# Chunked attention followed by a snake MLP on one core: another order of the words of the four MLP passes

## The chip, the cores and the metric

The kernel runs on one core of one Trainium2 chip. The metric is the device time of one execution in microseconds (us); lower is better. A profile is a separate execution, recorded by the hardware profiler; its span is the time from the first to the last recorded instruction, and the execution's own time is a little longer.

## The reference

Attention over four batches, eight heads, 768 positions of 64 values. Each chunk of 32 queries sees 8 memory rows, 16 positions to its left, itself and 8 to its right. The result, 3072 tokens of 512 values, goes through an MLP with a periodic activation.

```python
# attention, for each chunk c of 32 queries
k_full = np.concatenate([mem_k, k_ctx], axis=2)
v_full = np.concatenate([mem_v, v_ctx], axis=2)
scores = (1.0 / np.sqrt(64)) * np.matmul(q_c, k_full.transpose(0, 1, 3, 2))
a = np.exp(scores - scores.max(-1, keepdims=True))
out[:, :, c_start:c_end] = np.matmul(a / (a.sum(-1, keepdims=True) + 1e-09), v_full)
# MLP: x (3072, 512), w_in (512, 2048), w_out (2048, 512)
h = x @ w_in
s = np.sin(alpha * h)
g = h + s * s / (alpha + 1e-09)
return g @ w_out
```

## The kernel before

**Stages.** The program is a front and four passes. The front does the attention of batch 0. Pass i (0 to 3) does the MLP of batch i, and within it the attention of batch i+1 (pass 3 has none). The order of everything is written out by hand as five strings of words, `WORDS` (L21): the first is the front, the other four are the passes. `Stage.run` (L558) takes the words of a string one after the other and calls `do_` plus the first letter; the rest of the word is its argument. Each word emits instructions at the end of the queues of the engines that it uses. Every engine runs its own queue in order; between engines there are only the waits that the data ask for. So a word's place in the string sets its place in each queue.

**The MLP's first half.** The 2048 hidden values are 16 tiles of 128. For a tile n, `b` takes a pair of PSUM banks and does the matmuls of the first 384 columns, 4 of 384 columns each (L457), `h` the other 384 and then the sine on ScalarE (L472), `q` the square with the engine as its last letter (A is ScalarE at L477; V VectorE and P GpSimd, both at L480), and `g` the combination with the matmul result on VectorE (L484), which writes a slice of `gT` and gives the pair of banks back. There are four pairs. Tile buffers `u` and `s` are four deep as well.

**The second half.** `o` opens a feed of 96 matmuls of 512 columns (L495) for six blocks of 128 tokens, and `f` with a number takes so many from the feed. Whatever a pass leaves is taken at the end. After the 16 matmuls of a block, a copy out of PSUM (L502) on the engine that `e` names in turn, and an output transfer on SyncE's queue.

**The attention of the next batch.** `l` and `k` turn a quarter of q and k on TensorE (L312), `L` and `K` copy the results (L332, L323); these are for batch 1. Batches 2 and 3 have their k and q rows loaded by GpSimd's queue (`R`, with a count: L268 and L274 for k, L281 for q, 16 and 6 issues for a batch) into `kst` and `q_bf`, and crossed over by SyncE's queue (`X`, with a count: L296 to kT, L299 to qT, 8 and 6 for a batch). `V` loads a range of heads of v (batch, first head, last head); `m` and `H` put the memory rows of v into place (`H` by eight copies on GpSimd, L231), `Z` those of k. `s` with one to three digits does the scores of those blocks of 96 queries (L418) and the exponentials (three on ScalarE for a block, L432), `v` the values of one block (L447) and their normalisation on VectorE (L386, L387). The block is then transposed into `xT`, the input of the next pass, either by TensorE and a copy (`t` on VectorE, `T` on ScalarE, L399 and L402) or by a transfer on SyncE's queue (`c`, L666). The first column half of a tile needs blocks 0 to 3, the second blocks 4 to 7.

**The others.** `I` and `U` load pieces of w_in and w_out on GpSimd's queue. `W` (L738) is a one-element sine or exponential on ScalarE, which makes the engine load the table of that function there (ACT_TABLE_LOAD); without it, the table is loaded ahead of the first real sine or exponential. `d` loads rows for later batches.

**Slots.** PSUM banks, pairs and the six `x_blk` buffers are given out by the order in which they were returned (`Banks`, L95, and `Slots`, L81), so another order of words gives other banks too. Each of the two kinds of transfer queue has eight completion semaphores in rotation: an issue waits until the transfer eight issues earlier on it has landed.

Of the kernel before, what the change touches and what calls it, by code (L numbers as in the profile page):

```python
# [26 lines left out]
    ),  # L27
    (
# [5 lines left out]
    ),  # L34
    (
# [5 lines left out]
    ),  # L41
    (
# [5 lines left out]
    ),  # L48
    (
# [3 lines left out]
    ),  # L53
)

# [833 lines left out]
```

## Time and profile before

| what | us |
|---|---|
| median of 3 runs (lowest, highest) | 215.34 (215.27, 215.65) |
| the profiled execution's own time | 214.68 |
| its span | 212.8 |
| TensorE matmul busy (1772 instructions) | 204.9 |
| VectorE busy (210) | 139.9 |
| ScalarE busy (229) | 143.7 |
| GpSimd busy (142) | 100.9 |

The granted TensorE clock is 1.00 throughout. A matmul's record covers its whole way through the array, and matmuls overlap each other, so a busy TensorE does not show by itself that no time is lost. What tells is the time between the first matmuls of two stretches against the number of matmuls between them. The pieces of the chain of waits ("the chain that ended last") give such starts with counts. The front is before about 25 us; pass 0 begins at 24.8 us, pass 1 at 74.9, pass 2 at 121.5 and pass 3 at 167.6. The last 112 matmuls of the second half run from 188.8 us.

### The profile page before, as it was taken

To read this page: it belongs to the slowest core of one execution; us is meant where nothing else is said; L and a number is where in the kernel's file an instruction comes from. 1 tells how busy PE (TensorE), PEld (TensorE's weight loads), DVE (VectorE), ACT (ScalarE), POOL (GpSimd) and SP (SyncE) were. 2 spreads that over 40 slices of the span, in tenths; PEclk is the share of its full clock that TensorE was granted. 3 is DMA by queue.
4 is the path that set the end of the run, shared out by engine and by line. 5 is a ranking of instruction groups with operands and counts; after the bars stand their busy time and mean duration, and the time that the engine had idled before them with its cause. 6 is when DMAs were issued, how large, how long until landed. Compare 5 with 4: busy or idle time off the path is not lost.

```text
span 212.8 us, 4568 instructions
## 1 busy us (share of the span) xinstructions
PE 204.9 (96%) x1772; PEld 118.1 (55%) x1772; DVE 139.9 (66%) x210; ACT 143.7 (68%) x229; POOL 100.9 (47%) x142
## 2 busy tenths in 40 slices
PE   7879999999999999999999999999999999999994
PEld 7456665565455556555455555554555555554453
DVE  4788788999452749976766649897247187865010
ACT  2579898978848469968837199887856189891110
POOL 8998605589697297109795048664000022200000
PEclk9999999999999999999999999999999999999999
DMA  5999999999999999999999259999944400000312
GB/s 156 332 158 139 212 207 204 205 139 183 131 160 155 176 114 129 121 144 146 146 152 183 74 125 125 137 157 133 134 104 107 137 0 0 3 2 0 148 52 99
DMA packets 95853, 27.82 MB, mean 131 GB/s; under 512 B 84808, under 2 KB 92376, under 8 KB 95832
## 3 DMA queue, kind: packets, MB, share of 16 engines
q0 software_dynamic: 69152, 13.64, 89.3%
q1 hardware_dynamic: 25720, 12.68, 29.6%
q10 hardware_dynamic: 960, 1.21, 1.7%
q8 instruction: 14, 0.23, 0.6%
q14 instruction: 7, 0.06, 0.1%
HBM read 29.66 MB, written 6.29 MB: 169 GB/s over the span
## 4 chain that ended last, share of the span: by engine, by line
PE 78%; DVE 8%; ACT 5%; DMA 4%; issue 3%; SPq 1%; DVEq 0%; ACTq 0%
PE ps L495 39%; PE ps L457 30%; DMA kq_f<-in_k_dram 4%; PE ps L447 3%; DVE gT L484 2%; PE ps L418 2%; DVE x_blk L387 2%; DVE s L480 2%; ACT s L477 2%; PE ps L399 1%; ACT pt L365 1%; PE ps L312 1%; ACT u L472 1%; DVE q_bf L686 1%; DVE rinv L386 0%
## 5 line engine op out<-in xcount | busy, mean ns | idle before, releaser
L495 PE MATMUL ps<-w_out_sb,gT 128*128 128x512 bf16 (+1 forms) x400 | 89.1, 371 | 0.0
L457 PE MATMUL ps<-xT,w_in_sb 128*128 128x384 bf16 x512 | 85.9, 326 | 0.6 <-DVE gT L484 0.4
L484 DVE SCALAR_TENSOR_TENSOR gT<-s,inv_alpha,ps 128x768 bf16<-128x768 f32 x64 | 63.1, 1012 | 12.3 <-ACT s L477 5.2
L457 PEld LDWEIGHTS <-w_in_sb 128*128 128x128 bf16 x512 | 49.7, 98 | 35.2 <-issue 2.0
L472 ACT ACTIVATE u<-ps,alpha_sb 128x768 f32<-128x768 f32 x64 | 56.6, 894 | 16.9 <-PE ps L457 14.4
L495 PEld LDWEIGHTS <-gT 128*128 128x128 bf16 x400 | 37.1, 98 | 37.1 <-DVE gT L484 0.2
L480 POOL TENSOR_TENSOR s<-u 128x768 f32<-128x768 f32 x11 | 17.2, 1568 | 67.2 <-ACT u L472 56.4
L432 ACT ACTIVATE pt<-ps,biasm 128x256 bf16<-128x256 f32 x72 | 27.1, 488 | 10.5 <-PE ps L418 10.5
L502 DVE COPY o_sb<-ps 128x512 f32<-128x512 f32 (+1 forms) x15 | 10.0, 669 | 27.6 <-PE ps L495 25.7
L480 DVE TENSOR_TENSOR s<-u 128x768 f32<-128x768 f32 x23 | 21.9, 953 | 7.6 <-ACT u L472 7.5
L477 ACT ACTIVATE s<-u 128x768 f32<-128x768 f32 x30 | 25.0, 841 | 0.5
L387 DVE TENSOR_TENSOR x_blk<-ps,rinv 96x512 bf16<-96x512 f32 x32 | 22.0, 687 | 1.1
L502 ACT COPY o_sb<-ps 128x512 f32<-128x512 f32 (+1 forms) x10 | 5.7, 572 | 22.0 <-PE ps L495 22.0
L208 POOL DMA_DIRECT2D vw<-in_v_dram x13 | 12.0, 926 | 6.3 <-PE ps L399 5.4
L386 DVE RECIPROCAL rinv<-ps 96x8 f32<-96x8 f32 x32 | 6.4, 199 | 13.1 <-PE ps L447 12.7
L215 POOL DMA_DIRECT2D vw<-in_v_dram x13 | 13.3, 1024 | 1.6 <-DMA vw<-in_v_dram 1.6
L274 POOL DMA_DIRECT2D kst<-in_k_dram x16 | 13.0, 815 | 1.8 <-DMA vw<-in_v_dram 1.2
L268 POOL DMA_DIRECT2D kst<-in_k_dram x16 | 11.1, 691 | 2.1 <-DMA kst<-in_k_dram 1.0
L281 POOL DMA_DIRECT2D q_bf<-in_q_dram x12 | 10.7, 911 | 0.0
L402 ACT COPY xT<-ps 128x384 bf16<-128x384 bf16 x10 | 5.0, 496 | 8.2 <-PE ps L399 8.2
L447 PEld LDWEIGHTS <-pt 128*128 128x128 bf16 x192 | 8.2, 97 | 4.2 <-ACT pt L432 0.3
L447 PE MATMUL ps<-vw,pt 128*128 128x65 bf16 x192 | 8.9, 193 | 0.0
(83 smaller groups left out, 140.7 us busy)
## 6 DMA issues: line engine op xcount, KB each, us to landing
out_dram<-o_sb SPq DMA_DIRECT2D x23, 256.0 KB, 2.2
q_bf<-in_q_dram POOLq DMA_DIRECT2D x12, 128.0 KB, 7.7
kq_f<-in_k_dram SPq DMA_DIRECT2D x3, 384.0 KB, 6.2
kq_f<-in_q_dram ACTq DMA_DIRECT2D x3, 384.0 KB, 7.9
w_in_sb<-in_moe_w_in_dram POOLq DMA_DIRECT2D x1, 1152.0 KB, 12.9
vw<-in_v_dram POOLq DMA_DIRECT2D x7, 128.0 KB, 7.7
vw<-in_v_dram POOLq DMA_DIRECT2D x8, 112.0 KB, 8.1
kst<-in_k_dram POOLq DMA_DIRECT2D x14, 64.0 KB, 5.5
```

Source lines behind the costliest of these rows:

```text
L215: nc.gpsimd.dma_start(vw[72:128, c0:hi, 0:D], win(vflat, base + QW * c0 + 48, hi - c0, 56))
L274: nc.gpsimd.dma_start(kst[72:72 + n, j, :].rearrange("p (h d) -> p h d", d=D), k[b, :, QW * j + 48:QW * j + 48 + n, :].rearrange("h p d -> ...
L387: nc.vector.tensor_tensor(out=x_blk[:].rearrange("p g e d -> p e g d"), in0=otv[0:QW, :, :, 0:D], in1=rinv[:].unsqueeze(3).to_broadcast([Q ...
L432: nc.scalar.activation(pt[:, 0:H * QW].rearrange("p (g e c) -> p g e c", g=2, e=4)[:, :, :, 32 * m:32 * m + 32], sc[:, :, 0:4 * QW].rearra ...
L447: nc.tensor.matmul(otv[:, e, hp, :], pt[:, QW * i:QW * i + P], vws[b % 2][:, 2 * hp + e, j, 0:D + 1],)
L457: nc.tensor.matmul(t["hT"][:, hf, 0:HALF], w_in_sb[:, kt, P * t["ft"]:P * t["ft"] + P], t["xT"][:, kt, HALF * hf:HALF * hf + HALF], start= ...
L472: nc.scalar.activation(t["u"][:], t["hT"][:, :, 0:HALF], ACTF.Sin, scale=alpha_sb[:, ft:ft + 1])
L477: nc.scalar.activation(s2[:], u[:], ACTF.Square)
L480: e.tensor_tensor(out=s2[:], in0=u[:], in1=u[:], op=ALU.mult)
L484: nc.vector.scalar_tensor_tensor(out=gT[:, ft, :].rearrange("p (e c) -> p e c", e=2), in0=t["s2"][:], scalar=inv_alpha[:, ft:ft + 1], in1= ...
L495: nc.tensor.matmul(o[:, c0:c1], gT[:, ft, P * s:P * s + P], w_out_sb[:, ft, c0:c1], start=(ft == 0), stop=(ft == FT - 1),)
L502: copier(state["engines"][state["o"] % len(state["engines"])])(o_sb[:, c0:c1], o[:, c0:c1])
```

## The change

The four strings of the passes are replaced. The front's string and all functions are the same. TensorE does the same 1772 matmuls and the same number of every form. Counted over the program, ScalarE has 31 squares where it had 30, VectorE 20 where it had 23, and GpSimd 13 where it had 11; one of the K copies goes from VectorE to ScalarE and one copy of a transposed block from ScalarE to VectorE; 13 one-element activations become 8; the table is loaded 8 times in both. The tiles are opened (`b`) in the same order as before in all four passes; the second half of a tile (`h`) changes places with the next tile's `b` at a few (tiles 4 and 3 in pass 0, 7 and 11 in pass 1, 6 and 7, and 13 and 14 in pass 2). In pass 0 the squares stay with their engines, and `s70` goes ahead of `s61`. In pass 1, `R4` goes ahead of `V226`, the squares of tiles 11 and 13 go from ScalarE to GpSimd and that of 12 from GpSimd to ScalarE, and blocks 0, 5 and 1 are scored together. In pass 2, `H3` goes ahead of `R16`, `V305` goes ahead of `V357` and ahead of the square of tile 14; the squares of tiles 6, 9, 3 and 14 are GpSimd's and only those of 0, 2 and 12 VectorE's. In pass 3 the square of tile 6 goes from ScalarE to VectorE, that of 13 from VectorE to ScalarE and that of 15 from ScalarE to GpSimd.

```diff
--- before.py
+++ after.py
@@ -26,30 +26,28 @@
         'I02 Cs T00 v21 t10 T20 t31 z1 t11 I27 t21 Ws '
     ),
     (
-        'o8 b0 h0 I7g q0V U69 U12 b1 h1 dq108 q1A b4 h4 b3 g0 h3 b6 g1 dk108 q4V g4 q3A b2 h2 h6 b5 h5 Ufg g3 '
-        'b7 q2V U01 U56 q6P h7 g2 q5A b10 U24 q7P g6 h10 b9 q10A g5 h9 U45 b8 h8 g7 g10 q8A q9V V158 b11 h11 '
-        'g9 b13 g8 h13 l0 l2 l3 L0A L2A q13P k2 q11V Ube b15 U9b g11 Uef g13 K2V h15 b12 q15V h12 q12A b14 '
-        'g15 f7 h14 V125 k1 k0 g12 l1 K1V k3 L1V L3A q14V K3A K0A V102 dy f9 g14 s61 f16 m1 s70 s3 f13 v0 f3 '
-        'v6 Z2 c6 f6 v3 f5 s542 T3 f10 T0 v4 f6 v2 f2 v1 c4 c2 f7 v7 f1 T1 f3 v5 Ws T7 f8 t5 '
+        'I7g b0 U69 Ws h0 q0V dq108 b1 h1 o8 b4 b3 q1A h4 g0 g1 h3 q4V b6 dk108 q3A g4 U24 U12 b2 h2 h6 b5 g3 '
+        'h5 q2V b7 U01 q5A g2 U56 q6P h7 U45 b10 g6 h10 b9 g5 q7P q10A g7 h9 b8 h8 b11 g10 V158 q9V U9b q8A '
+        'h11 b13 g9 h13 l0 l2 g8 q13P Ube l3 Ufg L0A L2A q11V g11 g13 k2 b15 h15 b12 K2A q15V g15 h12 b14 '
+        'q12A Uef V125 h14 f7 l1 k1 g12 k0 K0A k3 K3A L3V L1A V102 q14V f9 K1V s70 g14 m1 f16 s61 s3 f11 v0 '
+        'dy v6 f8 c6 f1 v3 T0 f3 s542 T3 Z2 f11 v4 f9 c4 v2 v7 v1 f3 c2 f12 T1 v5 f6 t5 t7 '
     ),
     (
-        'b0 o1 h0 b3 R2 q0V h3 b1 Ws q3A g0 g3 h1 q1V b2 R4 h2 q2A b5 h5 b4 h4 Ws g1 g2 q5V g5 b6 q4A h6 R8 '
-        'Ws g4 b8 q6A g6 h8 R1 b9 q8V h9 b7 q9A g8 h7 R3 V378 b11 h11 V226 b10 g9 R4 h10 V202 V268 q7V Ws '
-        'q10A f2 X8 q11A g7 f8 b12 h12 g10 g11 b14 h14 q12P g12 b13 h13 q13A g13 q14A f7 X6 Z3 b15 g14 h15 f7 '
-        'eV We s24 q15V f6 g15 f7 s05 s1 f1 m2 f14 v4 v1 f6 v0 f1 v2 f2 c4 f6 s63 s7 t1 f4 c2 v6 T0 f4 v3 f4 '
-        'v7 c7 v5 t3 f17 t5 T6 '
+        'R4 b0 h0 o1 q0V b3 h3 q3A b1 h1 b2 h2 g0 g3 b5 q2A q1V R2 R1 h5 b4 g1 h4 g2 q5V b6 g5 q4A h6 b8 g4 '
+        'q6A h8 b9 g6 h9 q8V b7 R8 g8 q9A R3 b11 h7 V378 R4 h11 b10 g9 h10 f8 V268 q7V V226 V202 X8 q11P g7 '
+        'b12 q10A h12 g10 g11 b14 q12A h14 g12 b13 h13 f9 q14A q13P eV X6 g13 b15 h15 g14 q15V g15 f6 s24 f2 '
+        'Z3 f12 s051 m2 f10 v4 f7 v1 c4 f4 v0 s63 We T1 f6 v2 f4 s7 t0 v5 f8 v3 c2 f4 v6 v7 c7 t3 f16 t5 T6 '
     ),
     (
-        'b3 R16 H3 Ws b0 h0 h3 b5 h5 Ws b1 q5A q0V g0 q3P R6 g3 X4 h1 Ws q1A b2 h2 X4 g5 g1 b4 h4 b6 q4A q2V '
-        'h6 X2 g2 b7 h7 b9 h9 X1 g4 X1 q6V b8 g6 X2 eV o1 h8 q7P g7 q8A b11 h11 q11A q9P b10 g9 g8 h10 b13 '
-        'g11 h13 q10V g10 b14 h14 b12 q13P V357 V305 h12 g13 q12V q14A f8 eAV b15 g12 h15 f6 g14 q15V s24 f16 '
-        'g15 f2 s103 f9 v4 v0 f3 f2 c4 v3 f2 c3 v2 f1 c2 f6 c0 s675 f10 v1 f4 c1 Ws f1 v7 v5 c7 v6 f2 c6 c5 '
-        'f24 '
+        'H3 b3 b0 h0 h3 b5 h5 R16 q0V g0 b1 q3P o1 X4 q5A h1 b2 R6 q1A h2 g3 b4 g5 h4 g1 b6 q2V g2 q4A b7 g4 '
+        'h6 h7 X4 q6P b9 h9 b8 g6 q7A h8 g7 X1 b11 q8A q9P h11 eV X2 g9 q11A b10 g8 h10 q10A X1 b13 g11 b14 '
+        'h13 q13A b12 V305 g10 g13 h12 h14 q12V g12 f6 q14P V357 b15 h15 X2 q15A eAV f4 g14 We f4 s24 g15 f18 '
+        's103 f9 We v4 c4 f2 v0 c0 f3 v2 f4 We v3 f4 c3 c2 s675 f10 v1 f5 c1 v7 c7 v6 v5 c6 c5 f27 '
     ),
     (
-        'b2 h2 q2V b0 h0 b4 q0A g2 h4 b3 h3 g0 o2 b1 h1 Ws q3P b6 q4V q1A h6 g4 b8 h8 g3 b5 g1 q6A h5 q5A b7 '
-        'g6 h7 b11 q8P g8 h11 b10 g5 q7V h10 q10A q11P b9 h9 q9A g7 g11 b12 h12 b15 g10 q12A h15 g9 g12 b13 '
-        'h13 b14 q15A h14 g15 q14A q13V g14 g13 '
+        'b2 h2 b0 h0 q0A b4 q2V h4 g2 b3 h3 q3P g0 b1 h1 b6 q4V q1A h6 g4 b8 g3 h8 b5 h5 g1 o2 q6V q5A b7 g6 '
+        'h7 b11 q8P g8 g5 h11 b10 q7V h10 b9 q10A h9 g7 q11P q9A b12 h12 q12A g11 g10 b15 h15 g9 b13 g12 h13 '
+        'Ws q13A g13 q15P b14 h14 q14A g14 g15 '
     ),
 )
```

## The prediction

> **What bounds the kernel now.** I read the page's first lines, then the chain of waits, then the timelines of the places where it leaves TensorE.
>
> ```profile
> span 212.8 us, 4568 instructions
> PE 204.9 (96%) x1772; PEld 118.1 (55%) x1772; DVE 139.9 (66%) x210; ACT 143.7 (68%) x229; POOL 100.9 (47%) x142
> ```
>
> TensorE is the bound by its share, but a busy share does not say how much is lost inside. That comes from the chain, whose pieces give the start of a stretch, its length and its number of matmuls:
>
> ```profile
> 24.95 2.62 PE ps L457 x16
> ...
> 42.18 0.81 PE ps L312 x24
> ...
> 75.10 10.45 PE ps L457 x64
> ...
> 90.97 2.16 PE ps L495 x10
> ...
> 98.54 1.30 PE ps L457 x8
> ...
> 121.68 3.92 PE ps L457 x24
> ...
> 141.80 1.73 PE ps L495 x8
> ...
> 162.13 5.61 PE ps L495 x26
> 167.75 9.13 PE ps L457 x56
> ...
> 188.95 20.77 PE ps L495 x112
> ```
>
> Undisturbed, a matmul of the first half costs 1.30/8 = 0.1625 us and one of the second 5.61/26 = 0.216. Now the passes. Pass 3 goes from 167.75 to 188.95, 21.20 us for 16 tiles of 8 matmuls (20.80): 0.40 lost. Pass 2, 121.68 to 141.80 for 15 tiles (19.50): 0.62 lost. Pass 1, 75.10 to 90.97 for 12 tiles (15.60): 0.27. Pass 0, 24.95 to 42.18 for 13 tiles (16.90): 0.33. Together 1.6 us. The second half and the attention run at pitch in between, and the new order has as many matmuls of every form. So an order that is perfect from 25 us on gains 1.6 to 2 us (under 1%), and what it can lose has no such ceiling. The sum is therefore a sum of small waits, place by place. I number the passes as the code does and take times in the frame of the old trace.
>
> **Where pass 1 hands over to pass 2: the part I think decides.** The loads of batch 3's k rows (R16) and the copies H3 stand on GpSimd's queue, and the last block transfers of the attention on SyncE's:
>
> ```profile
> 95.51 1.46 POOL L480 TENSOR_TENSOR s<-u 128x768 f32<-128x768 f32 x1 [8.45 <-ACT u L472]
> 96.93 0.68 POOL L268 DMA_DIRECT2D kst<-in_k_dram  x1
> ...
> 109.73 0.63 POOL L274 DMA_DIRECT2D kst<-in_k_dram  x1
> 110.41 4.49 POOL L231 COPY vw<-memv_st 8x512 bf16<-8x512 bf16 x8
> ```
> ```profile
> 113.73 5.77 SPq L666 DMA_TRANSPOSE xT<-x_blk  x2
> 118.44 0.69 DVE L387 TENSOR_TENSOR x_blk<-ps,rinv 96x512 bf16<-96x512 f32 x1
> 121.52 3.25 PE L457 MATMUL ps<-xT,w_in_sb 128*128 128x384 bf16 x19
> ```
>
> Before, R16 follows the square of tile 12 at once, its 16 issues run from 96.93 to 110.36, and the copies come after. Now H3 stands first, and ahead of both the square of tile 13, which is the later tile: by the pitch its sine ends near 97.6, the square (1.46) near 99.1, the copies (4.49) near 103.6. So R16 runs from 103.6 to between 115.1 (0.72 each) and 117.0 (13.4 as before). How long such loads take to land, from the view of the tile kst between 96.5 and 111, and how long the block transfers (tile xT) took: first c4, issued at 110.00 among those loads, then c7, issued at 118.32 after them:
>
> ```profile
> DMA to landing us min/median/max: 4.2/6.6/7.9
> ...
> DMA to landing us min/median/max: 6.8/6.8/6.8
> ...
> DMA to landing us min/median/max: 2.3/2.3/2.3
> ```
> ```profile
> 114.00:116.00 2.00, 2.00 (x28) 1.17 (x27) 1.05 (x3) 2.00 (x7) 0.90 (x2) 1.00 1.42 158
> 116.00:118.00 2.00, 2.00 (x33) 1.29 (x29) 1.49 (x4) 0.95 (x3) 0.00 (x0) 1.00 0.39 94
> ```
>
> The windows (last columns but one: clock, DMA share) show the load traffic over by 117 (share 1.42, then 0.39), just before c7. In the new order the last loads land at about 115.1 + 6.6 = 121.7. And c7 itself is later: block 7 is now the last one normalised, behind block 3, an output copy and block 6. Counting back from the pass's start at 121.5 by matmuls (t5 and T6 0.3, f16 3.45, t3 0.2), the values of block 7 end at 117.55, where VectorE still has that copy (0.7, from 117.3) and block 6 ahead of it (0.7 and a reciprocal of 0.2, twice): its normalisation ends near 119.7, and c7 is issued there, 1.4 later than before. The second halves of pass 2's tiles read block 7; b3 and b0 still stand ahead of the first of them (h0), so TensorE asks for it at 121.52 + 8 x 0.1625 = 122.8. Landing after 2.3 us is 122.0: hidden. After 6.8 it is 126.5: 3.7 us lost. That is the pair of bounds. At the time that c7 is issued there are some 2 us of load traffic left where c4 had some 6.5 (110.00 to about 116.6), so I take a third of the way, 3.8 us, and a stall of 0.7; less a part because the loads have 16 crossing transfers fewer beside them than before: **0.5**. Block 2 (c2, issued near 114.2, needed at 121.5) lands by 121.0 even at 6.8. Everything behind h0 moves with it: the sines, the squares, R6. Nothing later gives it back.
>
> The Trainium skill (DMA: Bandwidth & Descriptors, Queues, rings and completion order) says that each DMA engine serves the queues it has work for in turn, a packet from each. By that a transfer beside one other busy queue takes about twice its time alone, as an estimate 4.6 us, which would make the stall 1.5 here. The 6.8 of c4 lies above that; no run here shows how the turns fall.
>
> **Pass 2 itself.** The last tiles before 141.8:
>
> ```profile
> 126.96 5.33 POOL L281 DMA_DIRECT2D q_bf<-in_q_dram  x6
> 129.09 1.01 DVE L484 SCALAR_TENSOR_TENSOR gT<-s,inv_alpha,ps 128x768 bf16<-128x768 f32 x1
> 130.67 0.84 ACT L477 ACTIVATE s<-u 128x768 f32<-128x768 f32 x1
> 131.42 1.69 ACT L472 ACTIVATE u<-ps,alpha_sb 128x768 f32<-128x768 f32 x2
> 133.99 1.02 DVE L484 SCALAR_TENSOR_TENSOR gT<-s,inv_alpha,ps 128x768 bf16<-128x768 f32 x1
> 135.06 3.00 PE L457 MATMUL ps<-xT,w_in_sb 128*128 128x384 bf16 x17 [0.16 <-DVE gT L484]
> ```
>
> b11 waited for the pair of tile 6 (g6, 133.99 to 135.01), whose square stood on VectorE. Now GpSimd squares tile 6, and h6 comes after b7. b7 needs g1 (ends 130.10), so it starts at 130.15, h6 ends at 131.45, the sine ends at 131.6 + 0.9 = 132.5, and GpSimd, free of R6 at 132.3, squares until 132.6 + 1.46 = 134.1. g6 then ends at 135.1, b11 starts at 135.2: **0.1 later**, not earlier. Further on ScalarE has nine squares instead of six: from tile 7 on it alternates sines and squares without a gap (about 0.8 each), the sine of tile 13 comes near 140.3, its square ends at 142.0, g13 at 143.05, and b15 waits for it where the matmuls would be ready at 143.0: another **0.1**. VectorE's three squares (0.95 each) are gone, which helps where it was the late engine (b9, b13), and TensorE meets the later b11 instead. I take +0.2. Bounds: -0.6 (all the pass's loss gone) and +0.6 (as much again). V305 now goes out at about 136, among the crossing transfers of q, of which the scores of blocks 2 and 4 near 146 need the first four:
>
> ```profile
> 134.55 4.34 SPq L299 DMA_TRANSPOSE qT<-q_bf  x3
> ...
> DMA to landing us min/median/max: 2.7/4.0/4.3
> ```
>
> Four of these are issued by 140.2 and landed by 144.5 at the slowest of their stretch, 1.6 ahead of the scores; beside loads they may take the 6.8 of c4, which is 147: no cost, with +1 as the bound.
>
> **Pass 3.** The place of its loss:
>
> ```profile
> 175.51 1.94 DVE L484 SCALAR_TENSOR_TENSOR gT<-s,inv_alpha,ps 128x768 bf16<-128x768 f32 x2 [0.24 <-POOL s L480]
> 177.76 0.83 ACT L477 ACTIVATE s<-u 128x768 f32<-128x768 f32 x1
> 178.62 2.86 DVE L484 SCALAR_TENSOR_TENSOR gT<-s,inv_alpha,ps 128x768 bf16<-128x768 f32 x3 [1.17 <-ACT s L477]
> 179.69 1.79 PE L457 MATMUL ps<-xT,w_in_sb 128*128 128x384 bf16 x10 [0.22 <-DVE gT L484]
> ```
>
> VectorE waited 1.17 us for ScalarE's square of tile 6. That square moves to VectorE, right behind its work ending at 177.45: 177.4 + 0.95, then g6 from 178.4 to 179.45, b11 at 179.5: **-0.2**, of the 0.4 lost. The next pairs then come in time. Bounds -0.4 and 0.
>
> **Pass 0.** Its first ten tiles keep VectorE's sequence; the quicker square of tile 5 saves one wait of 0.1 and the later h4 costs 0.1. Then the turns of q, which wait for pairs of tiles 9 and 8:
>
> ```profile
> 40.88 1.94 DVE L484 SCALAR_TENSOR_TENSOR gT<-s,inv_alpha,ps 128x768 bf16<-128x768 f32 x2
> 42.11 1.29 PE L312 MATMUL ps<-ident,q_bf 128*64 128x128 bf16 x36
> 43.01 1.49 ACT L332 COPY qT<-ps 128x768 bf16<-128x768 bf16 x2
> 75.21 0.36 DVE L402 COPY xT<-ps 128x384 bf16<-128x384 bf16 x1 [1.22 <-PE ps L399]
> ```
>
> g9 and g8 come 0.2 later, which costs under 0.1 as the next tile waits for ScalarE's two copies anyway; a third copy on ScalarE (K0, K3, L1 in a row) ends near 53.0, where the scores want it: 0.05; and two copies (t5, t7, 0.36 each) stand before the first h0 of pass 1 instead of one: 0.1. Sum **+0.2**, bounds 0 and +0.5. The sine's table, no longer asked for ahead by Ws, delays the first sine of pass 1 by 0.2, which its pair has in hand. **Pass 1** keeps VectorE's order up to tile 10 and with it its waits: 0.
>
> **The sum.** 0.5 + 0.2 - 0.2 + 0.2 = +0.7 on the profiled execution's 214.68, so 215.4 there. The median shown stands 0.66 above that execution; on the median's scale it is 215.34 + 0.7 = **216.0**.
>
> **The rivals.** (1) *The handoff is hidden and the rest cancels*: the loads land before c7, as the crossing transfers that slowed them (until 106) are done earlier. For it: 2.3 us is all that c7 took alone, with 0.8 in hand. Against it: 16 issues cannot end before 115.1. The time: 215.34 + 0.2 = 215.5. (2) *Faster*: in pass 2 the three squares taken off VectorE set free the pairs for which b9, b11 and b13 waited, and the pass runs at pitch; it decides at b11, if g6 ends before 134.8. Price: -0.6 there and -0.4 in pass 3, with the handoff hidden: 214.4 to 214.8. For it: VectorE's pieces stand in the chain all through that stretch. Against it: h6 behind b7, and GpSimd behind R6. (3) *The full handoff*: c7 takes what c4 took, or V305 holds up the transfers for the scores: +0.2 + 2 to 3.7, so 217.5 to 219. Against it: the loads' own traffic is near its end. That the change does nothing of what it says is excluded: every pass has another order on every queue.
>
> **How the numbers follow.** About 0.2% (0.43 us) is what a measurement of this kernel tells from no change. My case (slower by 0.45 to 1.6) has 0.48, rival 1 (within 0.43) 0.27, rival 2 0.16, rival 3 0.09. So faster 0.16, same 0.27, slower 0.57. My own case and rival 1 run from 215.1 to 216.9; to leave out no more than 2 in 10, the range takes rival 2's upper end and the bottom of rival 3: 214.8 to 217.4.
>
> **What would show it.** On the profile after: the k loads start near 103.6 and c7 is issued near 119.7 and lands after 122.8; a gap in TensorE's first-half matmuls after the first 8 of pass 2 (right), or none (rival 1). The first 13 tiles of pass 2 lose no less than before if my reading of tile 6 holds, and pass 3 loses 0.2 instead of 0.4. A pass 2 at pitch, or a long wait at the scores of blocks 2 and 4 in that pass, would make it wrong.

## The result, and the profile after

The changed kernel takes 216.2 us (median of 9 runs, 215.89 to 217.07) where the kernel before, run beside it, takes 215.1 (9 runs, 214.52 to 215.65). The ratio is 1.0058, with a 95% interval of 1.0039 to 1.0077: slower by about 1.25 us. The profiled execution took 216.2 with a span of 214.1.

First the head of the page of the changed kernel, whose line numbers are all two lower:

```profile
span 214.1 us, 4558 instructions
PE 205.6 (96%) x1772; PEld 118.2 (55%) x1772; DVE 135.7 (63%) x207; ACT 144.7 (68%) x225; POOL 104.6 (49%) x144
```

VectorE is busy 4.2 us less, GpSimd 3.7 more and ScalarE 1.0 more. These sums do not tell the time: TensorE is busy for 96% of the span before and after, and what it loses stands in its own rows. Here are the starts of the four passes and of the last second half, from the timeline of TensorE before (start, length, count):

```profile
24.78 1.47 PE L457 MATMUL ps<-xT,w_in_sb 128*128 128x384 bf16 x8
...
74.94 1.83 PE L457 MATMUL ps<-xT,w_in_sb 128*128 128x384 bf16 x10
...
121.52 10.66 PE L457 MATMUL ps<-xT,w_in_sb 128*128 128x384 bf16 x64
...
167.58 3.60 PE L457 MATMUL ps<-xT,w_in_sb 128*128 128x384 bf16 x21
...
188.78 3.40 PE L495 MATMUL ps<-w_out_sb,gT 128*128 128x512 bf16 x15
```

and after:

```profile
24.16 2.12 PE L455 MATMUL ps<-xT,w_in_sb 128*128 128x384 bf16 x12
...
74.31 2.49 PE L455 MATMUL ps<-xT,w_in_sb 128*128 128x384 bf16 x14
...
121.53 6.67 PE L455 MATMUL ps<-xT,w_in_sb 128*128 128x384 bf16 x40
...
168.09 0.81 PE L455 MATMUL ps<-xT,w_in_sb 128*128 128x384 bf16 x4
169.45 1.78 PE L455 MATMUL ps<-xT,w_in_sb 128*128 128x384 bf16 x10 [0.55 <-DMA xT<-x_blk]
...
190.02 2.32 PE L493 MATMUL ps<-w_out_sb,gT 128*128 128x512 bf16 x10
```

The differences of neighbouring starts, before and after: pass 0 50.16 and 50.15; pass 1 46.58 and 47.22 (+0.64); pass 2 46.06 and 46.56 (+0.50); pass 3 up to the last second half 21.20 and 21.93 (+0.73). Together +1.86. The front, whose code is the same, ended 0.62 earlier in the changed kernel's execution. In all the runs below whose profile is used, it ends between 23.9 and 25.3, so that is chance, and it is the reason why single executions are compared pass by pass here and not by their spans.

Next, where the chain of waits leaves TensorE in the changed kernel:

```profile
96.06 0.91 ACT u L470
96.97 0.07 issue
97.04 1.48 POOL s L478
98.54 1.94 DVE gT L482 x2
100.48 1.18 DVE s L478
101.71 0.04 issue
101.76 1.03 DVE gT L482
102.78 0.05 issue
102.83 1.68 PE ps L493 x7
...
138.82 7.77 DMA qT<-q_bf
146.59 0.14 issue
146.72 0.35 PE ps L416 x8
...
166.99 2.33 DMA xT<-x_blk
169.31 0.14 issue
169.45 8.62 PE ps L455 x52
...
183.75 1.02 DVE gT L482
184.78 0.04 issue
184.82 5.36 PE ps L455 x32
```

There are four places. In pass 1 TensorE waits for the pair of tile 15, behind VectorE's square of that tile, which took 1.25 us instead of 0.96 (0.36 lost by the time between matmuls). In pass 2 the scores of block 4 wait for a transfer of q that was under way for 7.77 (0.32 lost: from the first score to the next matmul of the second half it is 0.77 instead of 0.45). At the start of pass 3 the first second half waits for block 5: from the end of four matmuls, 168.09 + 4 x 0.1625 = 168.74, to 169.45, so 0.71. In pass 3 the wait for tile 6's pair fell from 0.38 to 0.16, and three tiles on a new one of 0.27 came.

What is missing is the wait on which the prediction rested. The 40 matmuls from 121.53 take 6.67 = 39 x 0.1625 and one matmul's own 0.33: no gap, through the first h0 and past it. Both halves of its cause are there, in the timelines of GpSimd and SyncE of the changed kernel:

```profile
98.57 5.22 POOL L229 COPY vw<-memv_st 8x512 bf16<-8x512 bf16 x8
103.74 0.70 POOL L266 DMA_DIRECT2D kst<-in_k_dram  x1
...
115.26 0.64 POOL L272 DMA_DIRECT2D kst<-in_k_dram  x1
```
```profile
119.67 1.19 SPq L664 DMA_TRANSPOSE xT<-x_blk  x1
```

The issues of the k loads start at 103.74, within 0.2 us of the forecast, and end at 115.9, between the two ends that it gave (115.1 and 117.0). Block 7's transfer is issued at 119.67, as forecast. The last load, issued at 115.26, landed 5.9 later, near 121.2, where 121.7 was forecast. So block 7's transfer did run beside the last of the loads, and it was in place by 122.8 all the same. In the first row the eight copies take 5.22 instead of the 4.49 of before; that belongs to the wait in pass 1.

### The profile page after: what moved, and what is told of

The parts are those of the page before. It is cut to its first block, busy times and chain, and to the rows that moved or that the text cites. A ratio compares the mean times of both kernels' runs of the same rounds, so it can differ in the third digit from the quotient of the medians.

```text
span 214.1 us, 4558 instructions
## 1 busy us (share of the span) xinstructions
PE 205.6 (96%) x1772; PEld 118.2 (55%) x1772; DVE 135.7 (63%) x207; ACT 144.7 (68%) x225; POOL 104.6 (49%) x144
## 4 chain that ended last, share of the span: by engine, by line
PE 60%; DVE 10%; SPq 9%; DMA 9%; issue 4%; ACT 4%; POOL 2%; DVEq 0%; ACTq 0%
PE ps L493 33%; PE ps L455 20%; SPq L294 5%; DVE gT L482 4%; DMA kq_f<-in_k_dram 4%; DMA qT<-q_bf 4%; PE ps L445 2%; DVE x_blk L385 2%; DVE s L478 2%; POOL s L478 2%; PE ps L416 2%; SPq L297 2%; ACT u L470 2%; PE ps L310 2%; ACT pt L363 1%
## 5 line engine op out<-in xcount | busy, mean ns | idle before, releaser
L478 POOL TENSOR_TENSOR s<-u 128x768 f32<-128x768 f32 x13 | 20.8, 1603 | 71.4 <-ACT u L470 61.7
L475 ACT ACTIVATE s<-u 128x768 f32<-128x768 f32 x31 | 26.1, 842 | 0.9
L478 DVE TENSOR_TENSOR s<-u 128x768 f32<-128x768 f32 x20 | 19.4, 969 | 8.4 <-ACT u L470 8.3
L400 ACT COPY xT<-ps 128x384 bf16<-128x384 bf16 x9 | 4.4, 484 | 14.3 <-PE ps L397 14.2
```

The costliest lines, as they stand in the source:

```text
L475: nc.scalar.activation(s2[:], u[:], ACTF.Square)
L478: e.tensor_tensor(out=s2[:], in0=u[:], in1=u[:], op=ALU.mult)
```

## The experiments

Each run was timed beside the kernel before. All ratios are to the kernel before, with a 95% interval. Lines of the edits are cut to the words around the change. A warm is a word `W`, the one-element activation that loads a table ahead of its use.

**One pass at a time.** The kernel before with one string of the four replaced by the new one (the first lines of each):

```diff
-        'o8 b0 h0 I7g q0V U69 U12 b1 h1 dq108 q1A b4 h4 b3 g0 h3 b6 g1 dk108 q4V g4 q3A b2 h2 h6 b5 h5 Ufg g3 '
+        'I7g b0 U69 Ws h0 q0V dq108 b1 h1 o8 b4 b3 q1A h4 g0 g1 h3 q4V b6 dk108 q3A g4 U24 U12 b2 h2 h6 b5 g3 '
...
-        'b3 R16 H3 Ws b0 h0 h3 b5 h5 Ws b1 q5A q0V g0 q3P R6 g3 X4 h1 Ws q1A b2 h2 X4 g5 g1 b4 h4 b6 q4A q2V '
+        'H3 b3 b0 h0 h3 b5 h5 R16 q0V g0 b1 q3P o1 X4 q5A h1 b2 R6 q1A h2 g3 b4 g5 h4 g1 b6 q2V g2 q4A b7 g4 '
...
```

> The kernel before with the new order of pass 0 alone. Theory A (the loss is a handful of separate waits, in the places where the two traces differ): the pass took 50.15 us in both traces, so 0.0 (within 0.2) on the kernel before. Theory B (the prediction's own sum): +0.2, at the turns of q and at the two copies ahead of pass 1.

> The kernel before with the new order of pass 1 alone. Theory A: the pass lost 0.64 us on the old one, of it 0.36 in one wait of TensorE for the pair of tile 15, some 0.2 because one run of scores is cut in two, the rest in the tiles. About 0.25 of the wait I put down to the memory-row copies (H3) that run beside VectorE's square of tile 15; here they come after the sixteen loads again, so that wait should be about 0.1: +0.3 to +0.4. Theory B (the prediction): 0. A third reading, that the wait comes from tile 13's square on GpSimd alone: +0.6.

> The kernel before with the new order of pass 2 alone (it holds H3 ahead of R16, the new place of V305 and the new order at the pass's end). Theory A: +0.35 at the scores of block 4, +0.15 in the tiles, +0.7 at the start of pass 3, and 0.1 to 0.25 at the pair of tile 15 in pass 1 by the copies beside VectorE's square: +1.2 to +1.4, with no wait at the first h0 of the pass. Theory B: +0.7, of it 0.5 in a wait for block 7 at the first h0. Theory C (the wait at the start of pass 3 was an accident of one execution, as the first transfer's issue took 2.33 us there): +0.6.

> The kernel before with the new order of pass 3 alone. Theory A: the wait for tile 6's pair (0.38) goes and two new ones of 0.16 and 0.27 come at the pairs that wait for tile 8's square on GpSimd: 0.0 (within 0.15). Theory B (the prediction): -0.2, the two new waits being due only to the late start of pass 3 in the changed kernel.

| string alone | median us | ratio |
|---|---|---|
| pass 0 | 214.55 | 1.0011 [0.9992, 1.0029] |
| pass 1 | 214.77 | 1.0009 [0.9989, 1.0029] |
| pass 2 | 215.91 | 1.0070 [1.0048, 1.0093] |
| pass 3 | 214.55 | 1.0019 [0.9995, 1.0042] |

The kernel before took 214.47 beside them. Only pass 2's string is slower by more than the measurement is uncertain, and by itself it is as slow as all four: 1.44 us by the medians, where theory A had 1.2 to 1.4. But the places were others than theory A had them, as the next rows show. In the traces pass 1 takes 46.91 with its new string, +0.33 on the 46.58 of before, as theory A said. The new pass 3 loses 0.18 and 0.27 at two tiles where the old lost 0.38 at one: theory A again, and not the prediction's -0.2.

Pass 2's string alone brought something that the changed kernel does not have. The timeline of ScalarE and TensorE in that run:

```profile
120.96 5.37 PE L456 MATMUL ps<-xT,w_in_sb 128*128 128x384 bf16 x32
...
123.14 1.28 ACT L471 ACT_TABLE_LOAD   x1 [1.51 <-PE ps L456]
...
127.50 0.81 PE L456 MATMUL ps<-xT,w_in_sb 128*128 128x384 bf16 x4 [1.18 <-DVE gT L483]
```

and ScalarE's in the changed kernel:

```profile
121.73 0.48 ACT L400 COPY xT<-ps 128x384 bf16<-128x384 bf16 x1 [6.59 <-PE ps L397]
122.23 1.28 ACT L470 ACT_TABLE_LOAD   x1
123.69 0.90 ACT L470 ACTIVATE u<-ps,alpha_sb 128x768 f32<-128x768 f32 x1 [0.17 <-PE ps L455]
```

The load of the sine's table (1.28) has no word of its own here, because the warm `Ws` ahead of the pass is gone. In the changed kernel it runs at once after a copy, while TensorE fills the first tile. In the other run the load itself carries the wait for TensorE (1.51): it starts 2.2 after the pass's first matmul instead of 0.7, and TensorE loses 1.34 ahead of its 33rd matmul (120.96 + 32 x 0.1625 = 126.16, to 127.50). Its scores did not wait afterwards, though q's transfers took 6.2 to 7.9 there: the tiles were late enough. The start of pass 3 lost 0.12 there and not 0.7.

**Mends of the changed kernel, one at a time.**

```diff
-        'H3 b3 b0 h0 h3 b5 h5 R16 q0V g0 b1 q3P
+        'R16 H3 b3 b0 h0 h3 b5 h5 q0V g0 b1 q3P
```

> The changed kernel with R16 ahead of H3 and of the pass's first tiles again (as before). Theory A: the copies no longer run beside VectorE's square of tile 15 in pass 1; that square takes 0.95 us again instead of 1.25 and TensorE's wait for the pair falls from 0.36 to about 0.1: -0.25 on the changed kernel. Theory B (the prediction: the loads cost at the handoff to pass 2): there was no wait at h0, so 0.0.

```diff
-        'b12 q10A h12 g10 g11 b14 q12A h14 g12 b13 h13 f9 q14A q13P eV X6 g13
+        'b12 q10A h12 g10 g11 b14 h14 q12P g12 b13 h13 f9 q13A q14A eV X6 g13
```

> The changed kernel with pass 1's squares of tiles 12 and 13 as before (12 on GpSimd, 13 on ScalarE). Theory A1 (the late square on GpSimd is the cause): tile 13's pair ends 0.2 to 0.3 earlier and so do those of 14 and 15; the wait of 0.36 goes to 0.1: -0.25. Theory A2 (the copies beside tile 15's square are the cause; they now start earlier, behind the square of tile 12): the square of tile 15 still takes 1.2, but starts earlier: -0.1 or less.

```diff
-        'h13 q13A b12 V305 g10 g13 h12 h14 q12V g12 f6 q14P V357 b15
+        'h13 q13A b12 g10 g13 h12 h14 q12V g12 f6 q14P V357 V305 b15
```

> The changed kernel with V305's two loads behind V357 again. Theory A: the transfers of q that run beside those loads take 3 to 4 us instead of 6 to 8, the scores of block 4 no longer wait: -0.35. Rival (the transfers are slow because they are issued in one row, whatever runs beside): 0.0, the wait stays.

```diff
-        v3 f4 c3 c2 s675 f10 v1 f5 c1 v7 c7 v6 v5 c6 c5 f27 '
+        v3 f2 v1 f2 c3 c2 c1 s675 f15 v7 c7 v6 v5 c6 c5 f27 '
```

> The changed kernel with the values of block 1 and its transfer moved ahead of the last scores of pass 2, so that SyncE has three transfers in the last row and not four. Theory A (SyncE's issuing, 1.2 us and more for each, binds the last transfer): the last one is issued 1.2 us earlier and the wait of 0.7 at the first second half of pass 3 goes: -0.6 to -0.7. Rival (block 5's normalisation, on VectorE behind those of 7 and 6, binds): 0.0. Third (an accident of one execution): the changed kernel beside it shows no such wait in most executions, so 0.0 and no wait in either.

| mend | median us | ratio |
|---|---|---|
| R16 ahead of H3 | 216.59 | 1.0098 [1.0070, 1.0126] |
| squares of 12 and 13 as before | 216.17 | 1.0087 [1.0064, 1.0111] |
| V305 behind V357 | 218.68 | 1.0199 [1.0164, 1.0234] |
| block 1 early | 216.92 | 1.0116 [1.0093, 1.0139] |

The kernel before took 214.64 beside them. The changed kernel was not timed again beside them; against its 1.0058 no mend came out faster, so none of the four gains that were expected is to be seen in the times. A gain of 0.25 us is 0.12%, which these intervals could not tell from none; what each mend did must be read from its trace. In their places they were half right, and the traces say why it did not help.

With R16 ahead of H3, VectorE's square of tile 15 takes 0.95 again and the wait of 0.36 is gone (pass 1 takes 46.91). The row, from the timeline of VectorE in that run:

```profile
100.41 0.95 DVE L478 TENSOR_TENSOR s<-u 128x768 f32<-128x768 f32 x1
```

and in the changed kernel:

```profile
100.40 1.25 DVE L478 TENSOR_TENSOR s<-u 128x768 f32<-128x768 f32 x1
```

So the cause of that wait is shown: the eight copies that GpSimd now makes beside it. With the squares of 12 and 13 put back, the copies end sooner, the square takes 1.05 and the wait goes as well. But then the scores of pass 2 waited 0.67 instead of 0.32 in the one run, and in the other ScalarE's table load drew the wait for TensorE again (1.34 lost at the start of pass 2).

With V305 moved back, q's transfers land fast and their wait is gone; but behind the late V357 its loads come too late for the values. The chain of that run:

```profile
148.01 1.21 POOL vw L206
149.22 7.32 DMA vw<-in_v_dram
...
156.67 0.43 PE ps L445 x8
```

TensorE lost 2.4 there, a cost that no theory of mine had: GpSimd's square of tile 14 keeps V357 until 145.2 in the new order. Ahead of V357, V305 slows q's transfers; behind it, it comes too late for the values.

With block 1 early, the wait at the start of pass 3 is gone, and a new one of 0.47 stands at the scores of blocks 6, 7 and 5, behind the normalisations that now crowd ahead of them. Up to there this kernel does what the changed one does, word for word, and its scores of block 4 waited 1.53 for q's transfers (landing 7.2 to 8.2) where the changed kernel's waited 0.32 (5.5 to 7.8). That wait varies from execution to execution.

**Then four kernels at the two causes left.** The new pass 2 alone with one warm put back; the changed kernel with three mends at once; the kernel before with edits meant to beat both; and the kernel before with nothing but V305 moved.

```diff
-        'H3 b3 b0 h0
+        'H3 b3 Ws b0 h0
```

> The new order of pass 2 alone again, with one table warm (Ws) put back ahead of the pass's second tile, where the old order has it. Theory: in the run without it the sine's table load (1.28 us) stood behind the first tile's matmuls (it started at 123.14, after ScalarE had waited 1.51 for TensorE), and TensorE lost 1.34 at 126.0; with the warm the load runs ahead of them, at about 122, and the kernel is 1.1 to 1.3 us faster than that run, so +0.1 to +0.4 on the kernel before (what V305 beside q's transfers costs is left). Rival (that wait has another cause, the loads' or copies' new order): +1.4 again, the wait of 1.3 stays.

```diff
-        'H3 b3 b0 h0 h3 b5 h5 R16 q0V
+        'R16 H3 b3 b0 h0 h3 b5 h5 q0V
...
-        'h13 q13A b12 V305 g10 g13 h12 h14 q12V g12 f6 q14P V357 b15
+        'h13 b12 q13P V357 V305 g10 g13 h12 h14 q12V q14A g12 f6 b15
...
-        f5 c1 v7 c7
+        f5 c1 Ws v7 c7
```

> The changed kernel with three mends: R16 ahead of H3 again; in pass 2 tile 13's square on GpSimd and V357, V305 behind it, as before, with tile 14's square on ScalarE; and one table warm ahead of the last values of pass 2. Theory (the copies beside tile 15's square in pass 1, and V305's loads beside q's transfers, are what the new order costs): in pass 1 the wait of 0.36 for the pair of tile 15 goes and the pass takes 46.9; q's transfers land after 3 to 4.5 us instead of 6.7 to 8.2, and the scores of blocks 2 and 4 don't wait; at the values of pass 2 no wait (V305 issued from about 143.5 again). Sum: -0.3 and -0.35 to -1.5, so 0.7 to 1.2 us faster than the changed kernel; +0.1 to +0.5 on the kernel before. Rival (transfers are slow by their own row, and the waits just move): no more than 0.3 faster than the changed kernel, +0.9 or more on the kernel before.

```diff
-        b1 Ws q3A g0
+        b1 q3A g0
...
-        b5 g1 q6A h5 q5A b7 '
-        'g6 h7 b11 q8P g8 h11 b10 g5 q7V h10 q10A
+        b5 g1 q6V h5 q5A b7 '
+        'g6 h7 q7A b11 q8P g8 h11 b10 g5 h10 q10A
```

> The kernel before with two edits. In passes 1 to 3 the seven table warms that come in mid-stretch, when the table is already loaded (0.18 to 0.20 us of ScalarE each, two of them in the chain of pass 2), are left out; in pass 3 the square of tile 6 goes to VectorE and that of tile 7 to ScalarE. Theory (the tiles' waits hang on single engines' rows of squares): b11 of pass 2 waits 0.1 to 0.2 less, b9 of pass 1 up to 0.1 less, and in pass 3 the wait of 0.38 becomes 0.16 without the 0.27 that the changed kernel has two tiles later, as VectorE gets one square and gives one away: -0.3 to -0.5 on the kernel before. Rival (each wait freed meets the next one): 0.0, within 0.2.

```diff
-        b11 h11 q11A q9P b10 g9
+        b11 h11 q11A q9P V305 b10 g9
...
-        b12 q13P V357 V305 h12 g13
+        b12 q13P V357 h12 g13
```

> The kernel before with one edit: V305's two loads go out behind tile 9's square (near 137, as in the changed kernel) instead of behind V357 (near 143.5). Theory (those loads slow q's transfers): the transfers of q in that stretch land after 6.5 to 8 us instead of 2.7 to 4.5, as in the five runs so far that have V305 there; the scores of blocks 2 and 4, asked for at 146.05, wait 0.3 to 1.5, and the kernel is 0.3 to 1.2 us slower than the kernel before. Rival (the slow transfers come from the new order's other parts, its row of SyncE issues or the later loads of k): transfers as before, no wait, 0.0.

| kernel | median us | before us | ratio |
|---|---|---|---|
| pass 2 alone with the warm | 215.72 | 214.39 | 1.0077 [1.0040, 1.0113] |
| three mends | 215.79 | 214.39 | 1.0079 [1.0052, 1.0106] |
| meant to beat both | 214.54 | 214.39 | 1.0008 [0.9989, 1.0028] |
| V305 early, all else before | 215.24 | 214.30 | 1.0047 [1.0019, 1.0076] |

The last run decides the matter of V305 in the kernel before. One edit makes the kernel before 0.94 us slower, and its view of q's transfers between 130 and 152 reads

```profile
L299 SPq DMA_TRANSPOSE qT<-q_bf x6: 1217/1241/1950, 133.8 to 141.2; - x6
...
DMA to landing us min/median/max: 7.6/8.1/8.1
```

against the 2.7/4.0/4.3 of the kernel before that the prediction shows. TensorE lost 0.67 between the scores of blocks 2 and 4. The chain of that run names VectorE's square there, because that ends at the same moment; the scores do not read it. The fourth transfer of q, issued at 138.49, landed 7.62 later, at 146.11, and the scores of block 4 began at 146.25, 0.14 after it. In the three other kernels whose scores waited (changed, R16 first, block 1 early) they began 0.13 or 0.14 after the landing too. Over all kernels the median landing in this view falls into two groups, with nothing between (of the six transfers the trace has the landing of three):

| V305 issued at | median landing of q's transfers, us |
|---|---|
| 135.9 to 137.6 (changed kernel, pass 2 alone, R16 first, squares 12 and 13, block 1 early, V305 early) | 6.7, 7.9, 7.1, 8.0, 8.1, 8.1 |
| 143 and later (before, passes 0, 1 and 3 alone, V305 back, three mends, meant to beat both) | 4.0, 4.5, 4.3, 3.5, 2.8, 3.0, 4.4 |

The other three fell. Putting the warm back did not make the new pass 2 faster (1.0077 after 1.0070): it is 1.33 us slower than the kernel before, which is what the rival said. That kernel has no profile from which rows could be read. It would fit that the scores, asked for 1.3 us earlier, then waited for q's transfers; that was not seen, so that the table load is the cause of the 1.34 rests on the rows above alone. The three mends came out 1.4 us slower than the kernel before, which is the rival's price (0.9 or more) and not the theory's. They did their parts (pass 1 46.93, transfers after 3.0, no wait at the scores), and the time went elsewhere: 0.57 at the start of pass 3, and in pass 2 tile 13's square, now GpSimd's, ends at 142.12, and TensorE waits for its pair, 0.72:

```profile
140.65 1.48 POOL s L478
...
142.15 1.03 DVE gT L482
...
143.22 1.46 PE ps L455 x8
```

The kernel that was meant to beat both is the kernel before within the uncertainty. Leaving out seven warms in mid-stretch changed none of the waits in pass 2 (0.14 and 0.32, as before), in pass 3 0.38 became 0.18 and 0.40, and pass 1's first scores waited 0.44 for a reason that stays open. No version was found that beats the kernel before.

**The wait at the start of pass 3.** Most of it looks like chance and not like the order, as the runs show side by side. SyncE issues the last four block transfers of pass 2 in a row; here is that row in the kernel before:

```profile
161.47 5.52 SPq L666 DMA_TRANSPOSE xT<-x_blk  x4
```

in the changed kernel, where the first of the four took 2.33 instead of 1.2:

```profile
161.97 6.23 SPq L664 DMA_TRANSPOSE xT<-x_blk  x4
```

and in the new pass 1 alone, which has the old order here:

```profile
161.68 5.82 SPq L665 DMA_TRANSPOSE xT<-x_blk  x4
```

TensorE lost 0.03, 0.71 and 0.31 behind them. In all twelve kernels with a readable profile that issue four in a row the wait is the length of this row less 5.5 us, to 0.02: with the old order 5.71 to 5.82 gave 0.20 to 0.31 in five kernels, with the new one 5.61 to 6.23 gave 0.10 to 0.71 in six. The profile of before, with 5.52, was the luckiest of them. Three of the six rows under the new order are longer than any under the old, so that the order has no part in it is not shown. What makes an issue long is open.

## Why the prediction was right, and where not

The time forecast was 216.0 and the time is 216.2, on the forecast side. As a difference, +0.66 was forecast and 1.25 measured (0.8 to 1.7 by the interval, of 215.1): the median of before fell by 0.24 with more runs. Term by term it is another sum, in which errors of both signs cancelled in part, so that it came so near is partly luck. By the signs that the prediction named for itself, its main part failed: no gap stands behind the first 8 matmuls of pass 2, pass 3 lost 0.4 again and not 0.2, and the scores of block 4 waited, if only 0.32.

*The handoff, +0.5: 0.* The steps before it held (loads from 103.74 for "near 103.6", c7 at 119.67 for "near 119.7"). What failed is the step "I take a third of the way, 3.8 us, and a stall of 0.7": block 7 was there by 122.8, so its transfer took under 3.2. The slow transfer that I measured it by, c4, stood among loads from its issue to its landing; only the last three loads landed after c7 was issued. The count in the step from 0.7 to 0.5 is wrong too: the trace of before has 14 crossing transfers in pass 1, and the last two of them were issued as these loads began (at 96.9 and 98.4), so there cannot be 16 fewer beside the loads. The loads did land sooner, after 4.2 at the median instead of 6.6. The estimate from the Trainium skill (DMA: Bandwidth & Descriptors, Queues, rings and completion order), 4.6 us and a stall of 1.5, is contradicted by the same rows. Rival 1 had it right that the handoff is hidden, but not why: the last load landed near 121.2, after c7 was issued.

*V305 beside q's crossings, 0 with a bound of +1: 0.32 in the changed kernel's profile, 0.94 as a single edit of the kernel before.* This is the step that failed on the other side. "Four of these are issued by 140.2 and landed by 144.5 at the slowest of their stretch" took the landing of the old trace, where these loads were not there; "beside loads they may take the 6.8 of c4, which is 147: no cost" names the right figure, and by it the scores at 146.05 would have waited. The bound was the better estimate. The third rival named this wait too, but priced it, like the full handoff, at 2 to 3.7.

*Pass 2's tiles, +0.2: about that* (0.50 less the 0.32 at the scores). Tile 6's square ended at 134.17 for "134.1", b11 began at 135.27 for "135.2".

*Pass 3, -0.2: 0.* The wait for tile 6 fell as said, by 0.22. "The next pairs then come in time" failed: VectorE has one square more up to there, and GpSimd's square of tile 8, which now runs beside it in part, takes 1.68 instead of 1.47, so that b12 waits 0.27.

*Pass 0, +0.2: 0* (50.15 and 50.16). *Pass 1, 0: +0.64 in the profile,* 0.33 of it with the new pass 1 alone (too little for the times to tell from none), 0.3 by H3 beside tile 15's square. That it "keeps VectorE's order up to tile 10 and with it its waits" was not wrong, but the copies that pass 2's string moves forward run in pass 1, and I asked only what they delay on GpSimd's queue, not whom they run beside.

*The start of pass 3* was not in the sum. The row of issues differs by 0.6 between kernels with the same words there (5.61 to 6.23), so most of it belongs to the scatter of this kernel.

What is shown: V305's place, moved alone in the kernel before, costs 0.94 us (0.4 to 1.6 by the interval), and the copies beside tile 15's square cost 0.3 in their place. How much of the changed kernel's 1.25 each of them makes is not measured: its one profile has 0.32 and 0.3, and taking both away at once brought other waits in their stead. That the rest is pass 1's and pass 2's tiles follows from the trace alone. The passes' ratios do not add up to 1.0058 (their excesses sum to 1.09%); a wait of 1.34 that the run of pass 2's string has and the changed kernel has not may be one reason.

## What to carry to other kernels

When a load is moved, price it by the transfers that it will run beside, with the landing times that the trace shows for such company, and not by those of the place it came from. When an order has waits of a few tenths on four queues, a mend of one is worth nothing by itself until the next wait behind it is known: here four local mends each took their wait away and none came out faster. A term whose bound is worked out from the nearest row, and whose likeliest value is set to nothing by hand, should be read again.

## What the runs showed of the hardware

A float32 square on VectorE and copies on GpSimd slow each other. VectorE's square of tile 15 in pass 1 took 1.25 in all three kernels that have the new pass 1 and the copies beside it from start to end, 0.95 or 0.96 where the copies come later, and 0.98 in the new pass 2 alone, where they overlap too. In these four kernels the eight copies took 5.22 instead of 4.49. With the squares of 12 and 13 as before only the end of the last copy overlaps: the square took 1.05 and the copies 4.49. The Trainium skill (SBUF — State Buffer, SBUF: two separate sides) says that the two engines share a pair of ports, which one holds for a whole instruction where a VectorE operation reads two operands from SBUF and GpSimd's reads SBUF too. By that a copy waits for the square (0.73 more), and the square at most for the rest of a copy of 0.56 (0.3, 0.1 or 0.03 here): the rows agree. VectorE's other operation, which reads PSUM and one such operand, took 1.00 to 1.02 beside GpSimd and alone.

q's transposing transfers land after about twice the time when V305's loads run beside them (medians of 2.8 to 4.5, and 6.7 to 8.1 with V305). Here the rule of the Trainium skill (DMA: Bandwidth & Descriptors, Queues, rings and completion order), a packet from each queue in turn, agrees.

The table load of ScalarE (1.28) can take over the wait of the sine that follows it, and then it is no longer hidden: in two kernels it began only after 1.51 of waiting for TensorE, and TensorE lost 1.34 there, while with the same words at that place the changed kernel lost nothing. That the load causes the 1.34 is read from the rows; the run with the warm put back was no faster.
